# v of the last three layer-1 chunks by seven products for eight, with the sums of its weights made in layer 1's first chunk

## The chip, the cores and the metric

The kernel runs on one core of one Trainium2 chip. The metric is the device time of one execution in microseconds (us). The engines are TensorE (PE, with PEld for its weight loads), VectorE (DVE), ScalarE (ACT), GpSimd (POOL) and SyncE (SP, which here issues most DMAs). They run beside each other, each in its own order, and wait for each other by semaphores.

## What is computed

Two layers share their weights. Each is a dilated local attention (32 heads of 32 channels, 8 positions back in steps of 2), then a SwiGLU block, both with a layer norm ahead and the input added behind. The sizes are 2048 tokens, 1024 channels and 3584 hidden channels, in bf16.

```python
def _A_ref(x, wqkv, wo):
    B, S, D = x.shape
    H = 32; Dh = D // H
    W, dil = 8, 2
    qkv = (lambda x, *d: x.transpose(*d))((x @ wqkv).reshape(B, S, 3, H, Dh), 2, 0, 3, 1, 4)
    q, k, v = qkv[0], qkv[1], qkv[2]
    ...
    logits = jnp.einsum("bhsd,bhswd->bhsw", q, kg) * scale
    logits = jnp.where(mask[None, None, :, :], logits, -1e9)
    attn = _softmax(logits, axis=-1)
    o = jnp.einsum("bhsw,bhswd->bhsd", attn, vg)
    return (lambda x, *d: x.transpose(*d))(o, 0, 2, 1, 3).reshape(B, S, D) @ wo

def _B_ref(x, w1, w3, w2):
    gate = jnp.einsum("bsd,df->bsf", x, w1)
    up = jnp.einsum("bsd,df->bsf", x, w3)
    h = _silu(gate) * up
    return jnp.einsum("bsf,fd->bsd", h, w2)

x = A_x
x = x + _A_ref(_layernorm(x, axis=-1), A_wqkv, A_wo)
x = x + _B_ref(_layernorm(x, axis=-1), B_w1, B_w3, B_w2)
x = x + _A_ref(_layernorm(x, axis=-1), A_wqkv, A_wo)
x = x + _B_ref(_layernorm(x, axis=-1), B_w1, B_w3, B_w2)
```

## The kernel before

**Stages.** The 2048 tokens are cut into four chunks of 512. A pair of layer and chunk is a unit; there are eight, numbered 0 to 7. First q, k and v of all four chunks of layer 0 are computed. Then come the eight units in turn: each has a B stage (the SwiGLU block of its chunk), and behind the B stages of units 1 to 4 stand q, k and v of one chunk of layer 1 (chunk 0 behind unit 1, chunk 3 behind unit 4). Attention itself runs beside this, in half chunks of 256 tokens, nearly all on DVE: score_steps multiplies q and shifted k (L590) and folds the products in a tree (L510 to L514), a softmax follows (L623 to L637), the weights go through POOL's DMA into At, and value_steps does the same with v (L665). Its result oT is multiplied by wo on PE in o_tile (L771, tiles po) and added to x.

**q, k and v.** q_part computes one of the three for one chunk: 64 matmuls with 512 columns into eight PSUM tiles ps (L836), each of which ACT evicts (L840) into a staging tile that goes to DRAM. It takes its weights with a step of eight columns (`t::KT`), which gives the head order that attention wants. Product tiles come from a pool of six PSUM banks; a pool of two more serves po, L and the small size sums.

**Seven products for eight.** In units 2 to 7 w1, w3 and w2 are multiplied by a scheme of Strassen's kind: both factors are cut in half each way, and seven products of sums of the halves replace eight. pipeline (from L1034) does w1 and w3: for each group of weights the products P1, P5, P6, P2 use the tile early and P7, P3, P4 the tile late; P7, P3 and P4 of a group stand between the first products of the next one, and behind the last group the first products of w2 are put between them (`fill`). The pass needs sums of the activations, made on DVE by norm_sums (L298), the last of them in place in xnT; a copy of P1 (L1064), one of P5 (L1069) and one of P6 (L1073) on ACT; and two additions on DVE, L1076 before P3 and L1088 or L1090 before P4.

**Sums of the weights.** They are made once, in units 0 and 1, while w1, w3 and w2 are multiplied in the plain way there. ACT squares each tile for its size (weight_size, L878; for w2 measure2, L958, on pieces loaded in layer 0's q, k and v), a matmul with a tile of ones adds over partitions (L892, L993), scale_of makes a power of two, ACT writes scaled fp16 copies into one of two blocks (L910, L1009), DVE forms the differences (L923, L1015), and POOL's DMA stores them to DRAM (t_d, t2_d). A weight tile is released for the next load when its copies have been queued.

**Order.** The order of PE, DVE, ACT and SP is written out by the program itself, with a clock of its own for each engine (`now`) and a price for each step. Queues hold work for the idle time of an engine: DVE takes from makes, norms, adds, values and scores in background(until), ACT from acts, sizes, parts and reads in act_background. A step is taken when it would end, by these clocks, within the time given. The clocks know of no PSUM banks. Some steps are forced: part_of_w2 takes from the head of `sizes` until all pieces of w2 so far are measured, then loads the next piece; ready_norm and o_tile force norms and attention. The layer norm of units 3 to 7 and of layer 1's chunks 1 to 3 is done by act_norm on ACT (L318 for the moments, then seven small steps on POOL, then L345), and two DMA transposes per half write xnT.

```python
    def act_background():
        for queue in (acts, sizes, parts, reads):
            while True:
                s = head(queue)
                if s is None or max(now["act"], s[1]) + s[0] > now["pe"] + gate[0]:
                    break
                take_act(queue)
```

Weights go through six buffers (wp) in the order of the list `seq`; a buffer is loaded again when it has been released (release, flush).

## Time and profile before

| | |
|---|---|
| median of three runs | 1533.16 us (1532.79 to 1533.34) |
| the profiled execution | 1532.7 us, its span 1531.0 us |
| DVE busy | 1201.8 us, 78% |
| ACT busy | 884.1 us, 58% |
| POOL busy | 153.7 us, 10% |
| granted clock of PE | 1.00 |
| DMA | 439.56 MB, mean 287 GB/s |
| layer 0's q, k and v | 25 to 192 us |
| B stages of units 0 and 1 | 192 to 514 us |
| layer 1's q, k and v | 514 to 556, 701 to 742, 885 to 927, 1073 to 1114 us |

The profile comes from one execution. Its groups give a line, an engine, an operation and tiles (output, arrow, inputs) with the count, the total busy time and the mean of one. The rows of a timeline have the start in us, the length in us, then engine, line and operation; equal neighbours are merged into one row with a count, and idle time ahead stands in brackets with what ended it. The chain of waits is followed back from the last instruction to what released it, and is shown here in order of time. Granted clock 1.00 means that PE was not throttled.

Durations of single operations that the change adds or moves, from the groups: the square of 2048 columns on ACT takes 1.90 us and 0.19 us for its accumulated sum (L878); a scaled copy of 512 columns 0.71 us (L910); a difference of 512 fp16 columns on DVE 0.42 us (L923); a sum of activations 0.69 us (L298); L1076 takes 0.70 us, L1088 0.75 us, an eviction L840 0.59 us.

### The profile page before, as it was taken

The numbers are of one execution on the slowest core, as the hardware profiler recorded it, in microseconds if no ns is written. First come the engines' busy times: TensorE is split into PE (matmuls) and PEld (weight loads), VectorE is DVE, ScalarE is ACT, GpSimd is POOL, SyncE is SP. The second block draws the span as 40 slices with busy tenths as digits, with TensorE's granted clock in tenths as the row PEclk, the third lists the DMA queues.
The fourth block names the chain that finished last, engine by engine and source line by source line (L and its number), as shares of the span: only waits on it lengthen the run. The fifth ranks groups of instructions, "written<-read, shape, count | busy, mean of one in ns | idle before, by whom it ended". The sixth has DMA issues, their size and how long they took to land.

```text
span 1531.0 us, 25095 instructions
## 1 busy us (share of the span) xinstructions
PE 1518.1 (99%) x9594; PEld 989.5 (65%) x9634; DVE 1201.8 (78%) x2126; ACT 884.1 (58%) x1388; POOL 153.7 (10%) x308
## 2 busy tenths in 40 slices
PE   9999999999999999999999999999999999999999
PEld 7666644444444577575786767766677767686865
DVE  4688998889989898989698958898678986435445
ACT  3885476567665357455565564756557445554643
POOL 1210102121211101001011010100111000000000
PEclk9999999999999999999999999999999999999999
DMA  9777969798997888979779997898969988878885
GB/s 321 202 218 215 253 226 330 272 304 289 306 320 247 280 316 294 347 264 303 263 269 324 346 268 282 280 323 302 323 225 333 338 296 282 306 272 334 318 294 203
DMA packets 261432, 439.56 MB, mean 287 GB/s; under 512 B 73856, under 2 KB 201088, under 8 KB 245056
## 3 DMA queue, kind: packets, MB, share of 16 engines
q1 hardware_dynamic: 248464, 390.90, 76.8%
q0 software_dynamic: 12704, 46.93, 8.6%
q8 instruction: 75, 1.23, 0.3%
q14 instruction: 45, 0.37, 0.1%
q10 hardware_dynamic: 144, 0.13, 0.0%
HBM read 345.90 MB, written 67.90 MB: 270 GB/s over the span
## 4 chain that ended last, share of the span: by engine, by line
PE 97%; ACT 1%; issue 1%; DVE 0%; DMA 0%; SPq 0%; ACTq 0%
PE st L1052 32%; PE ps L836 21%; PE w L1165 16%; PE po L771 7%; PE pg L1279 6%; PE pu L1288 6%; PE acc L1310 6%; PE pq L444 1%; PE L L604 0%; DMA wqkv<-in_A_wqkv_dram 0%; ACT L629 0%; ACT L1227 0%; ACT E L629 0%; ACT sg L1227 0%; DVE x_sb L1150 0%
## 5 line engine op out<-in xcount | busy, mean ns | idle before, releaser
L836 PE MATMUL ps<-xnT,wqkv 128*128 128x512 f16 (+1 forms) x1469 | 320.4, 379 | 0.2
L1052 PEld LDWEIGHTS <-early 128*128 128x128 f16 x2688 | 262.6, 98 | 40.4 <-issue 3.5
L836 PEld LDWEIGHTS <-wqkv 128*128 128x128 bf16 x1472 | 210.6, 144 | 108.1 <-issue 2.2
L1165 PE MATMUL w<-t,hT 128*128 128x512 f16 x1008 | 226.0, 379 | 0.6 <-ACT big L1185 0.5
L1052 PEld LDWEIGHTS <-late 128*128 128x128 f16 x2016 | 197.2, 98 | 30.6 <-issue 2.5
L590 DVE TENSOR_TENSOR tree<-qT,kT 128x2048 bf16<-128x2048 bf16 x128 | 156.3, 1221 | 35.8 <-DMA kT<-qkv_d 18.2
L1052 PE MATMUL st<-xnT,late 128*128 128x256 f16 x1344 | 174.2, 273 | 2.2 <-ACT big L1073 2.2
L510 DVE TENSOR_TENSOR tree<-tree 128x1024 bf16<-128x1024 bf16 x256 | 175.6, 686 | 0.9
L1052 PE MATMUL st<-big,early 128*128 128x256 f16 x1344 | 172.3, 273 | 1.6 <-ACT sg L1227 1.1
L1165 PEld LDWEIGHTS <-hT 128*128 128x128 f16 x1008 | 98.2, 98 | 112.9 <-DVE hT L1136 2.0
L1052 PE MATMUL st<-xnT,early 128*128 128x256 f16 x1344 | 165.7, 273 | 0.0
L665 DVE TENSOR_TENSOR tree<-At,vT 128x2048 bf16<-128x2048 bf16 x128 | 156.2, 1221 | 11.9 <-DMA At<-E 10.7
L1064 ACT COPY st<-st 128x512 f32<-128x512 f32 x84 | 48.3, 575 | 128.1 <-PE st L1052 127.4
L771 PE MATMUL po<-wo,oT 128*128 128x512 bf16 x486 | 110.8, 379 | 1.3
L840 ACT CAST hT<-ps 128x512 bf16<-128x512 f32 x96 | 55.8, 585 | 90.6 <-PE ps L836 88.3
L1288 PE MATMUL pu<-xnT,w3t 128*128 128x512 f16 x448 | 105.8, 379 | 0.0
L1279 PE MATMUL pg<-xnT,w1t 128*128 128x512 f16 x448 | 105.8, 379 | 0.0
L1310 PE MATMUL acc<-w2t,hT 128*128 128x512 bf16 x437 | 97.8, 379 | 0.6
L1076 DVE TENSOR_TENSOR st<-st,big 128x512 f32<-128x512 f32 x84 | 58.4, 695 | 46.9 <-ACT big L1073 46.8
L1227 ACT ACTIVATE sg<-st,down_scale 128x512 bf16<-128x512 f32 x126 | 86.6, 687 | 11.6 <-PE st L1052 11.0
L1052 PE MATMUL st<-big,late 128*128 128x256 f16 x672 | 87.1, 273 | 0.0
L771 PEld LDWEIGHTS <-oT 128*128 128x128 bf16 x512 | 50.1, 98 | 55.7
(167 smaller groups left out, 1916.6 us busy)
## 6 DMA issues: line engine op xcount, KB each, us to landing
early<-t_d SPq DMA_DIRECT2D x84, 1024.0 KB, 6.9
late<-t_d SPq DMA_DIRECT2D x84, 768.0 KB, 6.2
t<-t_d SPq DMA_DIRECT2D x42, 1024.0 KB, 7.3
t<-t_d SPq DMA_DIRECT2D x42, 768.0 KB, 5.3
wqkv<-in_A_wqkv_dram SPq DMA_DIRECT2D x28, 1024.0 KB, 8.1
w1t<-in_B_w_dram SPq DMA_DIRECT2D x14, 1024.0 KB, 7.6
w3t<-in_B_w_dram SPq DMA_DIRECT2D x14, 1024.0 KB, 11.0
t_d<-big POOLq DMA_DIRECT2D x28, 512.0 KB, 6.2
```

The costliest lines, as they stand in the source:

```text
L510: nc.vector.tensor_tensor(b, b, buf[:, 4:8, :], op=ALU.add)
L590: V.tensor_tensor(pr, qT[:], kT[:, :, k0:k0 + TCH], op=ALU.mult)
L665: V.tensor_tensor(tm.rearrange("p w (a e) -> p w a e", a=4), At[:].rearrange("p a w e -> p w a e"), win, op=ALU.mult)
L771: nc.tensor.matmul(ps[:], lhsT=oT[:, t, j * P:(j + 1) * P], rhs=wo[:, t, hh * 512:(hh + 1) * 512], start=(t == 0), stop=(t == KT - 1))
L836: nc.tensor.matmul(ps[:], lhsT=ws[kk // KH][:, kk % KH, t::KT], rhs=xnT[:, kk, :], start=(kk == 0), stop=(kk == KT - 1))
L1052: nc.tensor.matmul(out[:, a, :], lhsT=w[:, a, blk, k, :], rhs=rhs[:, k, :], start=start and a == 0 and k == 0, stop=k == KQ - 1, skip_grou ...
L1076: nc.vector.tensor_tensor(G["D"][:], G["D"][:], su, op=ALU.add)
L1165: nc.tensor.matmul(out[:], lhsT=lhs[:, k, j * P:(j + 1) * P], rhs=w[:, k, :], start=start and k == 0, stop=k == nq - 1, skip_group_check=True)
L1227: nc.scalar.activation(sg[:], src, ACTF.Silu, scale=inv)
L1279: nc.tensor.matmul(pg[:], lhsT=w1t[:, kk, fi * P:(fi + 1) * P], rhs=xnT[:, kk, :], start=(kk == 0), stop=(kk == KT - 1))
L1288: nc.tensor.matmul(pu[:], lhsT=w3t[:, kk, fi * P:(fi + 1) * P], rhs=xnT[:, kk, :], start=(kk == 0), stop=(kk == KT - 1))
L1310: nc.tensor.matmul(acc[:], lhsT=hT[:, f, j * P:(j + 1) * P], rhs=tiles[hh][f // nq][:, f % nq, :], start=(f == 0), stop=(f == f1 - f0 - 1))
```

## The change

v of layer 1's chunks 1, 2 and 3 is computed by pipeline, in two groups of four column tiles, instead of by q_part. A new function v_products sets it up: its results are scaled back and staged by ACT (and by L1088 for one quarter) and stored to qkv_d. The new t_dv in DRAM holds the sums of v's weights, and `seq` loads two early and two late tiles where it loaded the two v tiles.

The sums are made in layer 1's chunk 0: its order becomes v, q, k; v's two weight tiles are kept until q is done, and sums_of_v makes 16 scaled copies on ACT and 16 differences on DVE, in the second block and in a third one that lies in hT. Staging of that chunk has four slots for eight. The size of v's weights is measured by size_of_v: four squares queued in `sizes` ahead of q of layer 0's chunk 2, and one size sum. Sums of the activations are now also made for the keys of chunks 1 to 3 (sum_later in queue_q), the one in place only after k. In those chunks the point at which remaining po tiles are forced moves from ahead of v into v's first group.

Two more edits touch units 0 and 1. Sums of w2 are put in `reads` ahead of those of weights that are only prefetched. finish_sums lets DVE work on up to the time at which ACT's next step is ready.

```diff
--- before.py
+++ after.py
@@ -215,14 +215,19 @@
     up_scale = const.tile([P, 2, NG], FP32, name="up_scale")
     down_scale = const.tile([P, 2, NG], FP32, name="down_scale")
     size2 = const.tile([P, 16], FP32, name="size2")
+    size_v = const.tile([P, 4], FP32, name="size_v")
+    down_v = const.tile([P, 1], FP32, name="down_v")
+    up_v = const.tile([P, 1], FP32, name="up_v")
     total = const.tile([P, 1], FP32, name="total")
     down2 = const.tile([P, 1], FP32, name="down2")
     up2 = const.tile([P, 1], FP32, name="up2")
     peak = const.tile([P, 3], FP32, name="peak")
     hsum = const.tile([P, HTN // 2, HT], FP16, name="hsum")
     h16 = hT[:].bitcast(FP16)
+    blocks += [hT[:, 9:16, :].bitcast(FP16).rearrange("p b (k c) -> p b k c", k=KT // 2)]
     t2_d = [dram.tile([P, 7, (b - a) // 2, 512], FP16, name=f"t2_d{i}") for i, (a, b) in enumerate(fsplits)]
     t_d = [[dram.tile([P, 14, KT // 2, P], FP16, name=f"t_d{m}_{g}") for g in range(NG)] for m in range(2)]
+    t_d += [[dram.tile([P, 14, KT // 2, P], FP16, name=f"t_dv_{g}") for g in range(2)]]
     qkv_d = [[dram.tile([P, KT, S], BF16, name=f"qkv_d{l}_{i}") for i in range(3)] for l in range(2)]
 
     def hp():
@@ -692,7 +697,9 @@
             else:
                 seq += [("w2", g0, nq, hh) for hh in range(2) for g0 in (f0, f0 + nq)]
         if 1 <= u and u + 3 < len(units):
-            seq += [("qkv", which, h) for which in range(3) for h in range(2)]
+            seq += [("qkv", which, h) for which in ((2, 0, 1) if u == 1 else (0, 1)) for h in range(2)]
+            if u > 1:
+                seq += [("early", 2, 0), ("early", 2, 1), ("late", 2, 0), ("late", 2, 1)]
     w_tiles, w_at, due, used = [], {}, [], [0]
 
     def load_weight(pieces=1):
@@ -729,7 +736,7 @@
             if rest[0]:
                 got = {}
                 parts.append([weight_size(*rest[0], w, at, got), None])
-                reads.append([weight_sums(*rest[0], w, got), None])
+                reads.append([weight_sums(*rest[0], w, got), None, rest[0]])
         w_at[len(w_tiles)] = at
         w_tiles.append(w)
 
@@ -786,7 +793,8 @@
         key = ("Q", *units[q])
         plain_left.add(key)
         queue_norm(key, units[q][1], range(R))
-        
+        if q > NCH:
+            adds.append([sum_later(key), None])
 
     def sum_later(key):
 
@@ -817,7 +825,7 @@
                 assert norms and head(norms) is not None
         return xnT_at[key]
 
-    def q_part(l, c, which, ws, then=()):
+    def q_part(l, c, which, ws, then=(), last=2, ring=8):
 
         ready = ready_norm(("Q", l, c))
         xnT = xnTs[("Q", l, c)]
@@ -828,7 +836,7 @@
             nc.vector.memset(kT[:, :, 0:HALO], 0.0)
         for t0 in range(0, KT, SG):
             i = (c * 3 + which) * KT // SG + t0 // SG
-            i = i % (7 if l == 0 else 8) * SG
+            i = i % (7 if l == 0 else ring) * SG
             sgt = big[:, i * CH:(i + SG) * CH].bitcast(BF16).rearrange("p (a t) -> p a t", a=SG) if l == 0 else hT[:, i:i + SG, :]
             for t in range(t0, t0 + SG):
                 ps = bank("ps")
@@ -847,16 +855,16 @@
             nc.sync.dma_start(qkv_d[l][which][:, t0:t0 + SG, c * CH:(c + 1) * CH], sgt)
             landed = dma(256, done)
             if l == 0:
-                stored[:] = landed, landed
+                stored[0:2] = landed, landed
             if first and t0 == SG:
                 first_at = load_part(qT, 0, 0, 0, False)
             between(False)
             if t0 // SG < len(then) and then[t0 // SG]:
                 then[t0 // SG]()
         qkv_at[l, c, which] = landed
-        if which == 1:
+        if which == last:
             plain_left.discard(("Q", l, c))
-        if which == 2:
+        if which == last and last != 1 or (l, c, which) == (1, 0, 1):
             xnT_free["Q", l, c] = now["pe"]
         if first:
             qks[0, 0] = qT, kT, max(done + 0.1, first_at)
@@ -913,29 +921,63 @@
             makes.append([differences(m, g, a, now["act"] + 0.1), None])
         made.add((m, g))
 
-    pending, stored, made, held = [0] * 2, [0.0] * 2, set(), []
+    pending, stored, made, held = [0] * 3, [0.0] * 3, set(), []
     junk = hsum[:].bitcast(BF16).rearrange("p k t -> p (k t)")
 
-    def differences(m, g, a, r):
-
-        b = blocks[a]
+    def differences(m, g, a, r, slot=None):
+
+        slot = a if slot is None else slot
+        b = blocks[slot]
         for out, x, y in ((4, 5, 1), (1, 1, 0), (2, 4, 0), (6, 3, 2)):
             yield 0.40, r, lambda: nc.vector.tensor_tensor(
                 b[:, out], b[:, x], b[:, y], op=ALU.add if (x, y) == (4, 0) else ALU.subtract)
-        pending[a] -= 1
+        pending[slot] -= 1
         nc.gpsimd.dma_start(t_d[m][g][:, 4 * a:4 * (a + 1)], b[:, 0:4])
         nc.gpsimd.dma_start(t_d[m][g][:, 8 + 3 * a:8 + 3 * (a + 1)], b[:, 4:7])
-        stored[a] = now["dve"] + 7.0
+        stored[slot] = now["dve"] + 7.0
+
+    got_v = {}
+
+    def size_of_v(i, w, at):
+
+        w_ = w[:].rearrange("p k c -> p (k c)")
+        half = w_.shape[1] // 2
+        for j in range(2):
+            yield 1.95, at, lambda: nc.scalar.activation(junk, w_[:, j * half:(j + 1) * half], ACTF.Square,
+                                                         accum_out=size_v[:, 2 * i + j:2 * i + j + 1])
+        if i == 1:
+            total_scale(size_v, up_v, down_v, got_v)
+
+    def sums_of_v(ws, at):
+
+        while "at" not in got_v:
+            yield "blocked"
+        stored[2] = at
+        for g in range(2):
+            for a in range(2):
+                while pending[1] and pending[2]:
+                    yield "blocked"
+                slot = min((i for i in (1, 2) if not pending[i]), key=lambda i: stored[i])
+                pending[slot] += 1
+                b = blocks[slot]
+                for i, (kh, fh) in ((0, (0, 0)), (1, (0, 1)), (3, (1, 0)), (5, (1, 1))):
+                    t = 4 * g + 2 * fh + a
+                    yield 0.65, max(at, got_v["at"], stored[slot]), lambda: nc.scalar.activation(
+                        b[:, i], ws[kh][:, :, t::KT], ACTF.Copy, scale=up_v[:])
+                makes.append([differences(2, g, a, now["act"] + 0.1, slot), None])
+        made.add("v")
 
     def finish_sums(done):
 
         while not done():
-            if head(reads) is not None:
-                take_act(reads)
-            elif head(parts) is not None:
-                take_act(parts)
+            step = head(reads) or head(parts)
+            if step is not None:
+                background(step[1])
+                take_act(reads if head(reads) is not None else parts)
             elif head(makes) is not None:
-                take(makes)
+                background(head(makes)[1])
+                if head(makes) is not None:
+                    take(makes)
             else:
                 pe_requests(1, True)
 
@@ -1000,7 +1042,7 @@
 
     def sums_of_w2(i, f, ws, loaded):
 
-        while "at" not in got2 or all(pending):
+        while "at" not in got2 or all(pending[0:2]):
             yield "blocked"
         a = min((i for i in range(2) if not pending[i]), key=lambda i: stored[i])
         pending[a] += 1
@@ -1116,6 +1158,42 @@
                     if fill and i == n and tail != "P4":
                         fill(int(tail == "P3"))
             done(i)
+
+    def v_products(l, c):
+
+        key = ("Q", l, c)
+        slots, landed = [0], []
+
+        def stage(G, pair):
+            if ("to", pair) not in G:
+                i = slots[0] % 8 * SG
+                slots[0] += 1
+                G["to", pair] = hT[:, i:i + SG, :]
+                G["left", pair] = 2
+            return G["to", pair]
+
+        def consume(G, q, src, r):
+            pair, t0 = q % 2, HT * (q // 2)
+            to = stage(G, pair)
+            if q != 3:
+                nc.scalar.activation(to[:, :, t0:t0 + HT], src, ACTF.Copy, scale=down_v[:])
+                r = act(0.57, r)
+            G["left", pair] -= 1
+            G["at", pair] = max(r, G.get(("at", pair), 0.0))
+            if not G["left", pair]:
+                t = 4 * G["g"] + 2 * pair
+                nc.sync.dma_start(qkv_d[l][2][:, t:t + SG, c * CH:(c + 1) * CH], to)
+                landed.append(dma(256, G["at", pair]))
+                if len(landed) == 4:
+                    qkv_at[l, c, 2] = max(landed)
+
+        groups = []
+        for g in range(2):
+            G = dict(m=2, g=g, inv=down_v[:])
+            G["corner"] = lambda G=G: stage(G, 1)[:, :, HT:CH]
+            groups.append(G)
+        pipeline(key, groups, consume, lambda i: between(False, i == 0), True)
+        xnT_free[key] = now["pe"]
 
     def products(u, f0, f1, hold):
 
@@ -1316,7 +1394,8 @@
                         release_held(0)
                     if step == 0:
                         steps = range(u * nq // 2, (u + 1) * nq // 2)
-                        reads.extend([sums_of_w2(split, f, tiles, max(times[0] + times[1])), None] for f in steps)
+                        i = next((i for i, item in enumerate(reads) if item[2] not in held), len(reads))
+                        reads[i:i] = [[sums_of_w2(split, f, tiles, max(times[0] + times[1])), None, None] for f in steps]
                     act_background()
                     background(r + 1.0)
                     dve(0.64, r)
@@ -1360,6 +1439,9 @@
                 then = (None, None, lambda: (nc.sync.dma_start(wo[:], wo_v), dma(2048)))
             if c >= 1:
                 then = (then + (None,) * 3)[:3] + (part_of_w2,)
+            if (c, which) == (2, 0):
+                for i in range(2):
+                    sizes.append([size_of_v(i, w_tiles[4 + i], 40.0), None])
             q_part(0, c, which, w_tiles[2 * which:2 * which + 2], then)
             if c == NCH - 1:
                 release(2)
@@ -1375,11 +1457,27 @@
         with_q = 1 <= u and q < len(units)
         b_stage(u, with_q)
         if with_q:
-            for which in range(3):
-                if which == 2:
-                    between(False, True)
-                q_part(*units[q], which, [weight("qkv"), weight("qkv")])
+            if u == 1:
+                for which in (2, 0, 1):
+                    if which == 1:
+                        between(False, True)
+                    ws = [weight("qkv"), weight("qkv")]
+                    if which == 2:
+                        ready = max(w_at[used[0] - 1], now["pe"])
+                        reads.append([sums_of_v(ws, ready), None])
+                    q_part(*units[q], which, ws, (), 1, 4)
+                    if which == 2:
+                        continue
+                    if which == 0:
+                        finish_sums(lambda: "v" in made)
+                        release(2)
+                    release(2)
+                force(makes, lambda: not any(pending))
+                continue
+            for which in range(2):
+                q_part(*units[q], which, [weight("qkv"), weight("qkv")], (), 1)
                 release(2)
+            v_products(*units[q])
 
 
 # ---- launch: one core; inputs and outputs as the reference has them ----
```

## The prediction

> **What bounds the kernel now.** I read the page first, then the chain of waits in order of time, then who waits for whom on PE, and last the timelines of ACT and DVE where the change puts new work. The fences follow that order.
>
> ```profile
> PE 1518.1 (99%) x9594; PEld 989.5 (65%) x9634; DVE 1201.8 (78%) x2126; ACT 884.1 (58%) x1388; POOL 153.7 (10%) x308
> PE 97%; ACT 1%; issue 1%; DVE 0%; DMA 0%; SPq 0%; ACTq 0%
> ```
>
> PE is busy for 1518.1 of 1531.0 us and is 97% of the chain. A matmul taken off PE comes off the end, and a wait put before one goes onto it, nearly one for one. The chain also prices PE (start, length, what), where the spacing of starts counts and not the 379 or 273 ns of a pipelined matmul:
>
> ```profile
> 112.36 27.78 PE ps L836 x128
> ...
> 1072.65 41.44 PE ps L836 x192
> ...
> 1344.74 34.93 PE st L1052 x320
> ```
>
> A 512-column matmul of q, k or v costs 41.44/192 = 0.2158 us, a 256-column one of the seven-product pass 34.93/320 = 0.1092 us. The waits of PE show how little is lost (total, times, longest):
>
> ```profile
> PE st L1052 <- ACT big L1073: 2.2, 1, 2.2
> PE st L1052 <- ACT sg L1227: 1.1, 1, 1.1
> ```
>
> PE waits for no weights after the first 20 us. So ACT, DVE and DMA cost nothing today, and the question is where the change makes one of them late.
>
> ACT in layer 0's q/k/v, where the change puts its measuring:
>
> ```profile
> 122.91 0.58 ACT L840 CAST big<-ps 128x512 bf16<-128x512 f32 x1 [1.14 <-PE ps L836]
> 126.10 1.91 ACT L958 ACTIVATE hsum<-hT 128x2048 bf16<-128x2048 bf16 x1 [2.60 <-DMA hT<-in_B_w_dram]
> ...
> 128.14 1.91 ACT L958 ACTIVATE hsum<-hT 128x2048 bf16<-128x2048 bf16 x1
> ...
> 130.05 2.03 ACT L840 CAST big<-ps 128x512 bf16<-128x512 f32 x4
> ```
>
> Two squares stand between evictions; four products then wait, and PE doesn't. ACT at the end of k in layer 1 (unit 3), with the norm of the next B stage among the evictions:
>
> ```profile
> 913.28 0.58 ACT L840 CAST hT<-ps 128x512 bf16<-128x512 f32 x1
> 913.76 1.24 ACT L345 ACTIVATE xn<-x_sb,mom 128x1024 f16<-128x1024 bf16 x1
> 915.01 0.58 ACT L840 CAST hT<-ps 128x512 bf16<-128x512 f32 x1
> ```
>
> The first line evicts k's last product, the third v's first. L345 lies between at no cost, since v's first product needs 1.73 us.
>
> A seven-product pass starting (unit 5's B stage):
>
> ```profile
> 1113.93 1.04 PE L1052 MATMUL st<-xnT,early 128*128 128x256 f16 x8
> 1114.13 0.58 ACT L840 CAST hT<-ps 128x512 bf16<-128x512 f32 x1 [1.14 <-PE ps L836]
> 1114.80 1.36 PE L1052 MATMUL st<-big,early 128*128 128x256 f16 x11
> ...
> 1115.06 0.57 ACT L1064 COPY st<-st 128x512 f32<-128x512 f32 x1 [0.34 <-PE st L1052]
> ```
>
> P1 starts at 1113.93, P5 at 1114.80. P6 is due 1.75 us after P1 and needs the copy that ends at 1115.63, 1.70 after: 0.05 us of slack.
>
> **What the Trainium skill says.** "PSUM — Partial Sum Buffer", Specifications, gives 8 banks of 512 fp32; this kernel gives six to products, so six unread products stop PE. No run here shows PE stopped by that. "TensorE: Matmul & The Clock Gate", Architectural detail, says that ACT and DVE are strict FIFO; the trace agrees (the four late evictions at 130.05). "SBUF — State Buffer", Door 1, says that each step to a new 16-byte line pays, so reading every eighth bf16 should; the trace agrees for weight loads (144 ns for wqkv's strided tiles, 98 for early's) and shows no such read on ACT.
>
> **The change part by part.**
>
> *Removed and added on PE.* v of three chunks: 64 x 0.2158 = 13.81 us becomes 112 x 0.1092 = 12.23. Three times 1.58 is -4.75 us. One fp32 size matmul is added; the same at L993 shows 2 loads of 190 ns and 2 matmuls of 221: +0.5.
>
> *The measuring.* The change queues four squares of v's weights ahead of the next pair for w2. ACT's order in the built program shows all six together: after the eviction that stands at 122.91 come four squares, then the two L958, then eight evictions. They no longer wait until 126.10 for their data, as v's weights are there. So they start at 122.91 + 0.49 = 123.40; at 2.04 from start to start (126.10 to 128.14), five steps and 1.91 give 135.5, and the first eviction is over at 136.1. PE ends a product every 1.736 us; the one evicted at 122.91 ended at 122.78 (112.36 + 6 x 1.736), and the sixth after it at 133.2. Those six fill the six banks, so PE stands from 133.2 to 136.2: +3.0. PE is the bound from there to the end, and nothing later waits for anything that this time could cover. If the cover were one bank more it would be 1.3.
>
> *Start of the v pass.* ACT's order in all three chunks is: eviction of k's last product, L345, copy of P1 (L1064). With P1's start as zero, that eviction starts at 0.20, L345 runs from 0.68 to 1.92, the copy to 2.49. P6, due at 1.75, starts at about 2.53: 0.8 each, +2.4. Bounds: 0 if L345 is done before k ends, as the trace has it in unit 2 (726.98 to 728.12); 1.5 if its moments from POOL are late.
>
> *End of the v pass.* In a B stage P3 and P4 of a group are spread over the next group's products, and behind the last group w2's P1 fills in. The v pass has only two groups and no fill: P7, P3, P4 follow each other. P4 waits for L1088, which reads P7. Even with DVE free: 0.26 after P7, 0.75 of L1088, 0.05, against 0.87 of P3: 0.2. DVE isn't free in two chunks. Its order has the in-place sum of P7 (L298), which must wait for k's last matmul, then attention, then the adds of the pass and the four sums of the next B stage. With starts spaced as the trace spaces such neighbours (L665 to L512 1.13, L665 to L510 1.25, L510 to L665 0.72, L512 to L510 0.33, L298 to the next 0.6), the last L1088 ends 12.55 us after P1's start in chunk 1 and 13.45 in chunk 3; P4 is due at 13 x 0.873 + 0.8 = 12.15. That is 0.45, 0.2 and 1.35: +2.0. Bounds 0.6 and 4.
>
> *Edits hidden.* In layer 1's first chunk ACT makes 16 scaled copies. Contiguous ones (L910) take 0.71; strided I bound them by 0.71 and 1.4, so 11 to 22 us, and take 0.9. With 16 evictions of 0.585 and one exp of 1.9 that is at most 34 us in the 27.6 of v and q and two po tiles of 3.45: inside, as six banks carry a lag of 8 us; uncovered, the excess would fall on PE. The 16 DVE differences of 0.42 (6.7 us) delay attention, whose po tiles the order moves later too. The eight writes to DRAM on POOL have 100 us before they are read. The loads of unit 2's first weights move behind q's stores on SP, still 13.8 us ahead of use against the page's 6.9. A v pass loads 3.5 MB where 2 MB sufficed: early and late of v are issued a whole pass ahead; the next stage's first early is issued behind the second transpose on SP, some 2 to 4 us into the pass, 9 us before use, which covers the 6.9 by 2 only.
>
> *Reordered queues in units 0 and 1.* Sums of w2 go ahead of those of prefetched weights, DVE work is taken earlier, attention's q/k/v loads on SP come a few places later. The trace has 1 us of PE waits there to win; lost po or weights could cost 3. I take +0.5.
>
> Sum: -4.75 + 0.5 + 3.0 + 2.4 + 2.0 + 0.5 = +3.65 us. The profiled execution took 1532.7 us (span 1531.0 and 1.7 around it), 0.46 below the median 1533.16. So 1536.35 on its own scale, 1536.8 against the median.
>
> **Rivals.**
>
> A, not slower: DVE and ACT arrive early in the v passes, because PE comes 3 us late out of layer 0 while the order of the others was laid out without that hole; only the 0.2 for L1088 stays. -4.75 + 0.6 + 3.0 + 0.5 = -0.65, so 1532.5. It decides if the waits in the three passes sum to less than 1.8 us. For it: attention's results are some 2 us ahead of their po tiles in the trace. Against: L345 and the in-place sum are tied to k's end, not to a clock. 0.24.
>
> B: weights late. If the next stage's first early lands 2 to 3 us behind its use in each of three chunks, 1536.8 + 7 = 1544. For: DMA is 0.9 to 1.1 busy at the ends of these stages. Against: no wait of PE for weights in the whole trace. 0.09.
>
> C: ACT or attention late in units 0 and 1 or the first chunk (strided copies at 1.4, sums late for their release): +3, so 1540. 0.13.
>
> D: neither hole nor waits, 1528.9. It needs the squares to be spread. 0.03.
>
> **How the numbers follow.** The forecast has 0.51, its own range 1535.0 to 1538.8. No change is within 0.2% of 1533.16, that is 1530.1 to 1536.2, about what a measurement of this kernel can tell. The forecast gives 0.35 slower and 0.16 same; B and C 0.22 slower; A 0.22 same and 0.02 faster; D 0.03 faster. In all 0.05 faster, 0.38 same, 0.57 slower. The range 1532.0 to 1540.5 leaves out B, D and the ends.
>
> **What would show it.** PE in layer 0: one wait near 133 of about 3 us, released by an eviction (L840), behind six squares on ACT. In each v pass, P6 waiting for L1064 by 0.8, and the last P4 for L1088 by 0.2 to 1.4. PE's busy time about 4.3 less. Waits of PE on weights would mean B, on pg or po in units 0 and 1 C. No wait at 133 means that my count of banks or squares is wrong; passes of 12.3 us mean A.

## The result, and the profile after

The changed kernel takes 1558.93 us (median of four runs, 1557.54 to 1559.89), the kernel before in the same session 1533.25. The ratio is 1.0166 (95% interval 1.0148 to 1.0183): 25.7 us slower, where +3.65 was forecast. The profiled execution took 1558.95 us, its span is 1557.2. In the code after the change L836 is L844, L840 is L848, L1064 is L1106, L1073 is L1115, L1076 is L1118, L1088 is L1130 and L345 is L350.

The page's line of engines, after:

```profile
PE 1525.1 (98%) x9780; PEld 996.5 (64%) x9780; DVE 1223.8 (79%) x2171; ACT 919.6 (59%) x1424; POOL 158.1 (10%) x316
```

PE has less to do and is busy for longer. The view of what PE waited for, after (total, times, longest):

```profile
PE st L1094 <- DVE st L1118: 4.1, 3, 2.7
PE pu L1366 <- DMA w3t<-in_B_w_dram: 3.6, 1, 3.6
PE st L1094 <- ACT st L1106: 3.0, 3, 1.9
PE ps L844 <- ACT big L848: 2.9, 1, 2.9
PE acc L1388 <- DMA w2t<-in_B_w_dram: 2.4, 2, 1.5
PE st L1094 <- ACT hT L848: 2.0, 1, 2.0
PE po L778 <- DVE x_sb L783: 1.5, 1, 1.5
```

Past its first 20 us the kernel before had two waits over 1 us in this view; now there are these and some smaller ones, two of them on weights. All the waits in this view add up to 28.2 us against 7.0. That isn't all: after some gaps the granted clock of PE is half. Three stretches of the window view, after (PE, PEld, DVE, ACT, POOL busy, then the clock, the DMA share and GB/s):

```profile
120.00:150.00 30.00, 27.12 (x120) 16.43 (x119) 25.43 (x42) 21.76 (x30) 0.00 (x0) 0.94 0.68 191
462.00:484.00 22.00, 17.48 (x69) 7.05 (x67) 16.01 (x28) 15.07 (x22) 5.27 (x9) 0.84 1.07 365
565.00:600.00 35.00, 30.28 (x214) 23.54 (x213) 28.43 (x43) 17.23 (x27) 2.18 (x4) 0.95 1.06 367
```

The clock records show half clock for 3.41 us from 136.2, 6.83 us from 474.2 and 3.41 us from 586.8: 13.65 us at half speed. 1.3 us of them lie inside the wait for w3t, which ends at 475.5, so at most 6.2 us are lost. The kernel before has no such stretch until its end. The account of the span, +26.2: products -4.75 and the size matmul +0.5 (both from the prediction), waits +21.2, half clock +6.2. That is +23.2; about 3 us aren't placed.

By place: the first product of unit 0 is 4.1 us late, layer 1's first chunk 10.9, unit 2's B stage 21.0, and the rest adds 5. So most is lost before unit 2's B stage, where the v passes haven't begun. The delay of the chunk says too little of units 0 and 1: PE has lost some 17 us by then (12.8 in waits, 4.5 in half clock), but 32 matmuls of po that the kernel before did in these units now stand in the chunk, 7 us of it. That chunk takes 52.2 us for 42.1.

The first loss is the forecast one. ACT and PE in layer 0, timelines after:

```profile
122.11 0.59 ACT L848 CAST big<-ps 128x512 bf16<-128x512 f32 x1 [1.14 <-PE ps L844]
122.59 1.92 ACT L946 ACTIVATE hsum<-wqkv 128x2048 bf16<-128x2048 bf16 x1
...
132.78 1.91 ACT L1000 ACTIVATE hsum<-hT 128x2048 bf16<-128x2048 bf16 x1
...
134.69 2.52 ACT L848 CAST big<-ps 128x512 bf16<-128x512 f32 x5
```

```profile
135.31 4.87 PE L844 MATMUL ps<-xnT,wqkv 128*128 128x512 f16 x14 [2.88 <-ACT big L848]
```

Six squares in a row, then the late evictions; PE stands for 2.88 us. The v passes have waits at the start and the end, as forecast, but not of the sizes forecast. Chunk 1 on PE, then chunk 3 on PE and ACT:

```profile
756.57 1.03 PE L1094 MATMUL st<-big,early 128*128 128x256 f16 x8 [1.92 <-ACT st L1106]
...
765.98 1.03 PE L1094 MATMUL st<-big,late 128*128 128x256 f16 x8 [0.50 <-DVE st L1118]
767.77 1.03 PE L1094 MATMUL st<-xnT,late 128*128 128x256 f16 x8 [0.76 <-DVE hT L1130]
```

```profile
1128.98 1.03 PE L1094 MATMUL st<-big,early 128*128 128x256 f16 x8 [0.55 <-ACT st L1106]
...
1139.05 1.03 PE L1094 MATMUL st<-xnT,late 128*128 128x256 f16 x8 [0.30 <-DVE hT L1130]
```

```profile
1126.71 0.59 ACT L848 CAST hT<-ps 128x512 bf16<-128x512 f32 x1
1127.20 1.24 ACT L350 ACTIVATE xn<-x_sb,mom 128x1024 f16<-128x1024 bf16 x1
1128.34 0.59 ACT L1106 COPY st<-st 128x512 f32<-128x512 f32 x1
```

In chunk 3 L350 stands between k's last eviction and P1's copy, and P6 waits for the copy. In chunk 1 ACT has also waited 1.38 us for the moments of that norm from POOL.

### The profile page after: what moved, and what is told of

Read it like the earlier page. It is cut to its first block, busy times and chain, and to the rows that moved or that the text cites. A ratio compares the mean times of both kernels' runs of the same rounds, so it can differ in the third digit from the quotient of the medians.

```text
span 1557.2 us, 25585 instructions
## 1 busy us (share of the span) xinstructions
PE 1525.1 (98%) x9780; PEld 996.5 (64%) x9780; DVE 1223.8 (79%) x2171; ACT 919.6 (59%) x1424; POOL 158.1 (10%) x316
## 4 chain that ended last, share of the span: by engine, by line
PE 50%; DVE 10%; DMA 5%; ACT 4%; issue 2%; POOL 0%; DVEq 0%; ACTq 0%; POOLq 0%
PE st L1094 28%; PE w L1243 13%; PE po L778 5%; PE ps L844 4%; DVE tree L670 2%; DMA t_d<-big 2%; DVE tree L515 1%; DVE tree L595 1%; DMA w3t<-in_B_w_dram 1%; DMA xnT<-xn 1%; DMA late<-t_d 1%; DMA At<-E 1%; DVE tree L517 1%; DVE hT L1214 1%; DVE big L932 0%
## 5 line engine op out<-in xcount | busy, mean ns | idle before, releaser
L1094 PEld LDWEIGHTS <-early 128*128 128x128 f16 x2880 | 282.0, 98 | 44.5 <-issue 3.8
L844 PE MATMUL ps<-xnT,wqkv 128*128 128x512 f16 (+1 forms) x1280 | 281.4, 381 | 2.9 <-ACT big L848 2.9
L844 PEld LDWEIGHTS <-wqkv 128*128 128x128 bf16 x1280 | 183.4, 144 | 98.5 <-issue 7.3
L1094 PEld LDWEIGHTS <-late 128*128 128x128 f16 x2160 | 211.3, 98 | 40.1 <-issue 8.8
L1094 PE MATMUL st<-xnT,late 128*128 128x256 f16 x1440 | 187.1, 273 | 3.0 <-DVE hT L1130 1.3
L1094 PE MATMUL st<-big,early 128*128 128x256 f16 x1440 | 185.5, 273 | 3.0 <-ACT st L1106 3.0
L1094 PE MATMUL st<-xnT,early 128*128 128x256 f16 x1440 | 176.7, 273 | 2.0 <-ACT hT L848 2.0
L778 PE MATMUL po<-wo,oT 128*128 128x512 bf16 x512 | 116.2, 379 | 2.8 <-DVE x_sb L783 1.5
L1106 ACT COPY st<-st 128x512 f32<-128x512 f32 x90 | 51.8, 575 | 105.9 <-PE st L1094 105.0
L1118 DVE TENSOR_TENSOR st<-st,big 128x512 f32<-128x512 f32 x90 | 62.6, 696 | 48.4 <-ACT big L1115 48.3
L1094 PE MATMUL st<-big,late 128*128 128x256 f16 x720 | 93.7, 273 | 4.1 <-DVE st L1118 4.1
L1366 PEld LDWEIGHTS <-w3t 128*128 128x128 bf16 x448 | 44.1, 99 | 57.6 <-DMA w3t<-in_B_w_dram 4.1
```

The costliest lines, as they stand in the source:

```text
L778: nc.tensor.matmul(ps[:], lhsT=oT[:, t, j * P:(j + 1) * P], rhs=wo[:, t, hh * 512:(hh + 1) * 512], start=(t == 0), stop=(t == KT - 1))
L844: nc.tensor.matmul(ps[:], lhsT=ws[kk // KH][:, kk % KH, t::KT], rhs=xnT[:, kk, :], start=(kk == 0), stop=(kk == KT - 1))
L1094: nc.tensor.matmul(out[:, a, :], lhsT=w[:, a, blk, k, :], rhs=rhs[:, k, :], start=start and a == 0 and k == 0, stop=k == KQ - 1, skip_grou ...
L1118: nc.vector.tensor_tensor(G["D"][:], G["D"][:], su, op=ALU.add)
L1366: nc.tensor.matmul(pu[:], lhsT=w3t[:, kk, fi * P:(fi + 1) * P], rhs=xnT[:, kk, :], start=(kk == 0), stop=(kk == KT - 1))
```

## The experiments

"The plan" is the program's own clocks and prices, by which it writes out the order of the engines. Theories: T1, the two queue edits reorder units 0 and 1 and make weights late. T2, the squares in layer 0 cost by the stall, the half clock and the shift behind it. T2', the measuring costs because it moves the plan's clocks, whatever the instructions take. T3, making v's sums in layer 1's first chunk costs. "The chunk" below is that chunk.

**Queue edits and squares, each undone or done alone.** e1 is the kernel before with the first two of these edits; e2 takes them out of the changed kernel; e3 has the third; e4 is e2 and e3 together.

```diff
-                        reads.extend([sums_of_w2(split, f, tiles, max(times[0] + times[1])), None] for f in steps)
+                        i = next((i for i, item in enumerate(reads) if item[2] not in held), len(reads))
+                        reads[i:i] = [[sums_of_w2(split, f, tiles, max(times[0] + times[1])), None, None] for f in steps]
...
-            if head(reads) is not None:
-                take_act(reads)
+            step = head(reads) or head(parts)
+            if step is not None:
+                background(step[1])
+                take_act(reads if head(reads) is not None else parts)
...
-            if (c, which) == (2, 0):
-                for i in range(2):
-                    sizes.append([size_of_v(i, w_tiles[4 + i], 40.0), None])
+            if (c, which) == (3, 0):
+                then = (square, square, square, part_of_w2)
+            if (c, which) == (3, 1):
+                then = (square, None, None, part_of_w2)
```

> The kernel before with the change's two queue edits alone: background work before each step of the routine that finishes the sums, and the w2 sums put ahead of those weights' sums that are not held. Nothing of v is added. T1 (the queue edits put unit 1's w3t squares ahead of the w2 copies, so that weights come late in unit 1's second split and the clock halves there): 1541 to 1545 us, with PE standing some 4 us for w3t near 470 us of the span. T2 (the squares of v's weights in layer 0 start the loss: a hole of 2.9 us, half clock for 3.4 us, and everything after them shifted against the transfers): 1532.5 to 1534.5, no gap over 1 us in unit 1.

> The changed kernel with both queue edits undone. T1: unit 1's second split runs as before, its 9 us come back, 1547 to 1550 us. T2: the gap for w3t stays, 1557 to 1560. T3 (the making of v's sums in layer 1's first chunk costs most) says nothing on the queues: 1555 to 1559.

> The changed kernel with the four squares of v's weights taken one at a time, one after each second pair of blocks of q's and k's parts of layer 0's chunk 3, and not four in a row. T2: the gap of 2.9 us near 132 us and the half clock after it go (4.6 us), and unit 1's 9 us with them if it was the shift that put w3t late: 1545 to 1548. T1: only the 4.6 us: 1553.5 to 1555.5.

> Both of the last two: squares spread, queue edits undone. T1 and T2 each 1541 to 1545, since what either blames is gone; what then stands above the kernel before is the making of the sums in layer 1's first chunk (3 to 5 us, with the half clock after it) and whatever moved besides, less what the seven products save. If the losses do not add, over 1548.

e1: 1532.71 us, ratio 0.9997 (0.9989 to 1.0006). This run says less than it seems to: in the kernel before the queue edits leave every instruction where it was, so e1 is the same program once more. What they do in the changed kernel is seen in e4, where undoing them gives another order. e3: 1558.24 (ratio 1.0161). The stall at 132 us is gone, unit 0 starts at 191.7 us instead of 196.6, and everything is lost again by the end, so T2 falls as well. e4: 1557.74, so the loss is there with the queue edits and without them, and T1 falls. e2, which nobody had expected: 1672.26 (ratio 1.0901). The largest part stands in the chunk, where PE waits some 60 us for DVE: the differences of v's weights stand on DVE before attention's work, and DVE waits for ACT (timeline of e2). Another 22 us PE waits in units 0 and 1 for an ACT step (sg, L1359), which wasn't followed further.

```profile
591.88 1.68 DVE L932 TENSOR_TENSOR hT<-hT 128x512 f16<-128x512 f16 x4 [21.12 <-ACT hT L965]
```

The same undoing cost nothing in e4, with the squares elsewhere. Whether an order is good depends on everything else in the plan.

**Measuring apart from the sums.** e5 takes the measuring out and leaves v's scale a constant 32, so it doesn't follow the data; e6 also gives the strided copies their true price; e7 and e8 are the kernel before with the queue edits and the measuring alone, in a row or spread.

```diff
-    got_v = {}
+    got_v = {"at": 0.0}
+    nc.vector.memset(up_v[:], 32.0)
+    nc.vector.memset(down_v[:], 0.03125)
...
-                    yield 0.65, max(at, got_v["at"], stored[slot]), lambda: nc.scalar.activation(
+                    yield 1.26, max(at, got_v["at"], stored[slot]), lambda: nc.scalar.activation(
```

> The changed kernel without the measuring of v's weights: no squares, no size matmul, the scale of v's sums is the constant 32. Left out: the data-dependent scale. Up to layer 1's first chunk its instructions stand in the order of the kernel before. T2' (the four squares and the size matmul move the planner's clocks, so that it orders units 0 and 1 otherwise and the weights of unit 1 come late there): the 10.9 us that the changed kernel is late at layer 1's first chunk all come back, and no half clock near 474 us; 1545 to 1549 us. T1' (the weights of unit 1 are late for another reason): the gap near 470 us stays, over 1553. T3 (making the sums in layer 1's first chunk): what stays above the kernel before arises between 513 and 620 us of the span, 10 us or more.

> The last one with the strided copies of v's weights priced in the order-making plan at 1.26 us, what the profile shows, and not at 0.65. The instructions are the same, their order in layer 1's first chunk is not. T3a (the loss there is a plan made with a price that is half the real one: 16 copies, 10 us too few on ACT): the order fits, PE's waits of unit 2's first B stage go, 3 to 6 us under the last one. T3b (the work itself, 20 us of ACT and the differences on DVE in a stage of 42 us, is too much for the stage): within 2 us of the last one.

> The kernel before with the queue edits and the measuring of v's weights as the change does it (four squares in a row, the size matmul, the scale), whose result nobody uses. T2 and T2': at layer 1's first chunk some 11 us late, as the changed kernel is, and about that at the end: 1542 to 1546 us. If the changed kernel's loss in unit 1 needs v's products too: 1536 to 1538 (the hole and the half clock after it alone).

> The last one with the squares one at a time in layer 0's chunk 3. T2' (any change of the planner's clocks costs): no hole in layer 0, but unit 1's order is moved as in the changed kernel with spread squares, so 1541 to 1547. T2 (the hole is the cause): 1533 to 1535.

e5: 1539.39 (1.0040, 1.0025 to 1.0055), below what was expected. e6: 1532.85 (1.0003, 0.9994 to 1.0011), 6.5 under e5, where 3 to 6 was expected; PE's wait for DVE's addition in unit 2's B stage falls from 4.2 to 2.25 us and doesn't go. e7: 1553.66 (1.0136), e8: 1552.14 (1.0123), both above. So the measuring, which nobody uses in e7 and e8, costs some 20 us, and all of v's sums and products cost 6.3 us, or nothing with a true price. e7 also shows that unit 2's late start needs no strided copy: its B stage is 13.3 us late against the kernel before, of which the chunk has added 6.9.

The price, in groups of equal form, after (the last numbers: total, mean ns, idle before):

```profile
L918 ACT ACTIVATE big<-w3t,up_scale 128x512 f16<-128x512 bf16 x56 | 36.4, 711 | 19.6 <-DMA t_d<-big 18.0 <-DVE up_scale L878 1.6
...
L965 ACT ACTIVATE big<-wqkv,up_v 128x512 f16<-128x512 bf16 x8 | 9.9, 1272 | 0.0
L965 ACT ACTIVATE hT<-wqkv,up_v 128x512 f16<-128x512 bf16 x8 | 9.8, 1254 | 2.6 <-DMA t_dv<-hT 2.6
```

A copy that reads every eighth bf16 takes 1.26 us, one that reads neighbours 0.71, and the plan charges 0.65 and 0.61. Sixteen copies make ACT 10 us later than the plan thinks, and the differences behind them hold up DVE. PE after, at the start of unit 2:

```profile
577.33 1.05 PE L1094 MATMUL st<-xnT,early 128*128 128x256 f16 x8 [2.00 <-ACT hT L848]
...
586.34 1.46 PE L1094 MATMUL st<-big,late 128*128 128x256 f16 x8 [2.72 <-DVE st L1118]
```

**The plan apart from the instructions.** e9 keeps the whole plan of e7 and emits neither squares nor size matmul nor scale: it is the kernel before in another order, which is e7's. e10 does the reverse in the changed kernel. e11 is the changed kernel with 1.26 alone. e12 is the whole change, squares spread and unknown to the plan, with 1.26.

```diff
-            yield 1.95, at, lambda: nc.scalar.activation(junk, w_[:, j * half:(j + 1) * half], ACTF.Square,
+            yield 1.95, at, lambda: None
...
-            yield 1.95, at, lambda: nc.scalar.activation(junk, w_[:, j * half:(j + 1) * half], ACTF.Square,
+            yield 0.0, 0.0, lambda: nc.scalar.activation(junk, w_[:, j * half:(j + 1) * half], ACTF.Square,
```

> The measuring of v's weights in the plan alone: the order of all instructions is that of the run with the measuring in a row (1553.7 us), but the four squares, the size matmul and the five small DVE operations are not there. It is the kernel before, computing the same, in another order. If the order is the cause of what is lost in units 0 and 1: 1545 to 1551 us, with PE standing for w3t near 465 us of the span. If the squares and the stall and half clock that they bring are the cause: 1533 to 1536.

> The other half: the changed kernel with the four squares in a row and v's size real, but unknown to the plan, so that all else stands in the order of the run without measuring (1539.4 us). v's size goes through w2's size matmul (20 columns for 16). If the order is the cause: 1539.4 plus a stall in layer 0 of at most 2.9 and a half clock of at most 1.7, 1539.5 to 1544. If the squares are the cause: 1552 to 1559.

> The changed kernel with the strided copies priced at 1.26 us in the plan, and nothing else. If the losses of the measuring and of the price are independent: 1558.9 less the 6.5 us that the price was worth without measuring, 1551 to 1554. If the price was worth 6.5 us only in that order: anywhere from 1548 to 1560.

> The whole change, complete, with both mended: the four squares one at a time in layer 0's chunk 3 and unknown to the plan, the strided copies at 1.26. If the order is the cause, as without measuring and with the true price (1532.9 us): 1531.5 to 1534.5, the same as the kernel before or 0.1% under it. If the squares cost by themselves: 1536 to 1541. Faster than 1530.1 (0.2%) would mean that the v passes save their whole 4.75 us, which the last runs do not show.

e9: 1551.27 (1.0120, 1.0106 to 1.0133): 18 us slower without one added instruction. e10: 1540.48 (1.0051), 1.1 over e5: the squares themselves cost next to nothing (here four and two stand apart on ACT, and PE doesn't stall). e11: 1549.43 (1.0113), below the range for independent losses and inside the wider one. e12: 1535.40 (1.0020, 1.0011 to 1.0030), above its range and under that of the other theory. Its order is e6's but for the squares and the small DVE operations; near 215 us PE waits 2.77 us for such an operation (down_scale, L892), with half clock behind, which e6 doesn't. Of e9's 16 us (spans of the two traces), 9.1 are lost before unit 2's B stage and 6.9 in it. PE's two largest waits in e9 stand in these two places:

```profile
PE st L1070 <- DVE st L1094: 4.7, 1, 4.7
PE pu L1306 <- DMA w3t<-in_B_w_dram: 3.6, 1, 3.6
```

How an order makes weights late is seen in unit 1, at the second of them. SyncE's queue, before:

```profile
395.14 8.70 SPq L272 DMA_TRANSPOSE xnT<-xn  x4
...
409.68 4.05 SPq L727 DMA_DIRECT2D w1t<-in_B_w_dram  x1
413.83 3.29 SPq L727 DMA_DIRECT2D w3t<-in_B_w_dram  x1
```

and in e9:

```profile
382.70 17.32 SPq L725 DMA_DIRECT2D w2t<-in_B_w_dram  x2
402.53 12.44 SPq L275 DMA_TRANSPOSE xnT<-xn  x4
...
423.88 3.41 SPq L730 DMA_DIRECT2D w3t<-in_B_w_dram  x1
```

The load of w3t starts 10 us later, of which 2.6 are the delay of the whole stage. SyncE's order is nearly the same in both; its loads wait longer for their buffers. ACT, before:

```profile
435.22 1.33 ACT L1009 ACTIVATE big<-w2t,up 128x512 f16<-128x512 bf16 x2 [1.06 <-DVE x_sb L1324]
436.46 1.89 ACT L878 ACTIVATE hsum<-w3t 128x2048 bf16<-128x2048 bf16 x1
```

and in e9:

```profile
437.70 1.91 ACT L881 ACTIVATE hsum<-w3t 128x2048 bf16<-128x2048 bf16 x1 [9.39 <-DMA w3t<-in_B_w_dram]
...
441.64 4.99 ACT L1027 ACTIVATE big<-w2t,up 128x512 f16<-128x512 bf16 x8
```

The squares of w3t, a tile loaded ahead, stand before twelve of the sixteen copies of w2; in the kernel before fourteen of these come first. ACT waits 9.39 us for w3t with those copies behind it, the buffers come free late, and so does the next load. PE, in e9:

```profile
468.09 1.90 PE L1306 MATMUL pu<-xnT,w3t 128*128 128x512 f16 x8 [3.57 <-DMA w3t<-in_B_w_dram]
```

**Which entry of the plan.** The orders that the program writes out show it: 7.8 us charged to ACT for the squares leave the order as it was but for a few places on ACT, and the size matmul's slot on PE leaves it as it was. The 1.1 us charged to DVE for v's scale, alone, change everything behind; 1.0 alone still gives the old order on all engines but DVE, 0.9 on DVE too. Beside the squares' charge 0.9 already gives e9's order, and 0.2 doesn't. The five operations take 0.93 us in the trace (142.49 to 143.42 after). e13 charges 1.1 us to DVE in the kernel before with the queue edits and does nothing else; e14 is the changed kernel with 0.2; e15 is e14 with 1.26; e16 is e9 with the two squares of that w3t held back.

```diff
+        yield 0.0, 0.0, lambda: makes.insert(0, [iter([(1.1, now["act"] + 2.5, lambda: None)]), None])
...
-            yield 1.1, r, emit
+            yield (1.1 if n == 16 else 0.2), r, emit
...
-                parts.append([weight_size(*rest[0], w, at, got), None])
+                parts.append([weight_size(*rest[0], w, at + (9.0 if rest[0] == (1, 4) else 0.0), got), None])
```

> The kernel before with the queue edits, and 1.1 us charged once to VectorE in the plan, where the scale of v's weights would be made; no instruction is added, none left out. That charge alone gives another order of the instructions in units 0 and 1; a charge of 0.9 us, or 7.8 us charged to ScalarE for the squares, gives the order of the kernel before but for some places of single ScalarE instructions. If any order that comes from a shifted plan is worse than the tuned one: 1540 to 1555. If only the order of the last plan-only run is bad: 1531 to 1537.

> The changed kernel with one number of the plan changed: the five small VectorE operations that make v's scale are charged at 0.2 us and not at 1.1. All the instructions of the change are there. The SyncE and GpSimd orders become those of the run without measuring. If the loss in units 0 and 1 comes from this flip: 1539.4 and the hole with its half clock, 1540 to 1545. If the squares in a row matter beyond the hole: over 1550.

> The changed kernel with two numbers of the plan changed: the item of the last run at 0.2, and the strided copies at 1.26 us. If the two losses are what separates the changed kernel from the kernel before: 1532.9 (no measuring, true price) and at most 4.6 for the hole and the half clock after it, 1533 to 1538. If something else is lost: over 1541.

> The plan-only run (1551.3 us) with the two squares of the w3 weights of unit 1's second split held back in the plan by 9 us, so that they do not stand ahead of the w2 copies on ScalarE. If the strict order on ScalarE (copies behind squares behind a transfer that lands late) makes the weights of that split late: its PE gap of 3.6 us near 465 us goes, and 5 to 8 us with it, 1543 to 1547. If the transfers are late by themselves: 1550 to 1552. It moves other things too, so a number over 1552 would say nothing of this link.

e13: 1554.21 (1.0136, 1.0121 to 1.0152). Its order isn't that of e9, and its waits are others (PE in e13):

```profile
PE po L771 <- DVE down_scale L884: 5.1, 1, 5.1
PE po L771 <- DVE oT L514: 3.1, 4, 1.7
PE st L1058 <- DVE big L298: 2.5, 1, 2.5
PE acc L1316 <- DMA w2t<-in_B_w_dram: 2.5, 1, 2.5
```

Unit 2's B stage begins 20.5 us late here. So it isn't one bad order: another one that comes from a shifted plan is as bad. e14: 1543.64 (1.0078). One number takes 15 us off the changed kernel. Its order is e5's but for the added squares and small operations; it is 4.3 us over e5, and the stall of layer 0 is 2.87 of them. e15: 1539.01 (1.0038, 1.0024 to 1.0051), a little above its range. Two numbers take 20 us off. But 0.2 is no truer than 1.1. With 0.93, which is what the trace shows, and 1.26 for the copies, the program writes e11's order, instruction for instruction, and e11 took 1549.43. The 0.2 helps because it is too small to move the order. PE's waits in e15:

```profile
PE ps L844 <- ACT big L848: 2.9, 1, 2.9
PE st L1094 <- ACT big L1115: 2.2, 1, 2.2
PE st L1094 <- DVE st L1118: 1.8, 1, 1.8
```

The first is the stall of layer 0; no wait on w2t or w3t is left among the large ones. e16: 1544.23 (1.0076), 7.0 us under e9, and the wait for w3t isn't there any more. The squares ahead of the copies were that link, as far as one run tells that also moves other things.

**Towards a faster version.** In e6 ACT waits 4.56 us in the chunk for a store of v's part, which SyncE issues behind four transposes and four weight loads. e17 (e12) and e18 (e6) issue these stores from GpSimd.

```diff
-            nc.sync.dma_start(qkv_d[l][which][:, t0:t0 + SG, c * CH:(c + 1) * CH], sgt)
+            (nc.gpsimd if (l, c, which) == (1, 0, 2) else nc.sync).dma_start(
+                qkv_d[l][which][:, t0:t0 + SG, c * CH:(c + 1) * CH], sgt)
```

> The mended whole change (1535.4 us) with the four stores of v's part of layer 1's first chunk issued by GpSimd and not by SyncE, where they stand behind four transposes and four weight loads. If ScalarE's wait of 4.56 us for such a store is what makes VectorE late in unit 2's first B stage: PE's wait of 2.2 us there goes, and its half clock where there is one, 1531 to 1534. If VectorE is late by its own backlog: 1534.5 to 1536.5. Worse than 1537 would mean that GpSimd's queue, which also stores v's sums, is now the late one.

> The same store edit on the run without measuring and with the true price (1532.9 us), v's scale being the constant 32. First theory: 1529 to 1531.5, under the kernel before. Second: 1532 to 1534.

e17: 1534.98 (1.0020, 1.0013 to 1.0028). e18: 1533.20 (1.0001, 0.9993 to 1.0009). ACT no longer waits for the store (in e18 it waits 2.05 us for one of v's sums instead), but PE's wait for L1118's add only falls from 2.2 to 1.3 us (e12, e17) and 1.8 (e6, e18), and the times stay where they were. The store was part of DVE's lateness there; that the rest is DVE's own backlog was not traced. No version here beats the kernel before. From layer 1's chunk 1 to the end e6 is 2.9 us shorter than the kernel before, of the 4.75 taken off; unit 2's B stage before it gives 3.2 back.

## Why the prediction was wrong

**"Reordered queues in units 0 and 1 ... I take +0.5", bounds -1 to +3.** This step failed. It named the queue edits, and alone these move nothing (e1); with the squares spread, undoing them gains nothing (e4). It didn't ask what the measuring does to the order: a price added to the plan can move every decision behind it. The charge of 1.1 us on DVE for v's scale alone gives an order that costs 22 us, 20 of them before unit 2's B stage (e13); the measuring's whole charge costs 18, of which 9 are lost by then and 7 in that stage (e9). It read the new order only around the new instructions, not what else had moved in units 0 and 1, where the squares of w3t now stood ahead of twelve copies of w2. The rival C, with "sums late for their release", had this kind of lateness and its place, at +3 and 0.13, about a sixth of its size.

**"Edits hidden": nothing for the chunk.** Its bounds of 0.71 and 1.4 for a strided copy held the measured 1.26. But 0.9 was taken, and the sum on ACT was set against PE's time in the chunk as a whole. The plan's own price, 0.65, wasn't compared with it. The error of 10 us on ACT falls on the differences and the attention behind them on DVE. Mended, it is worth 6.5 us without measuring (e5, e6), 9.5 in the changed kernel (e11) and 4.6 beside the other number (e14, e15). These gains include what the new order brings, which the runs don't part from the price's own share.

**Not in the sum at all: the clock after a stall.** At most 6.2 us in the changed kernel, 1.7 of them behind the stall in layer 0.

**The stall in layer 0, +3.0.** Right: 2.88, released by an eviction behind six squares. The Trainium skill's "PSUM — Partial Sum Buffer", Specifications, had given the banks of which this kernel uses six, and the trace now shows PE stopped by them.

**Start and end of the v pass, +2.4 and +2.0.** Near in the sums, not in the parts, so in part luck. P6 waited 1.92, 0.55 and 0.55 us, 3.0 in all, where 0.8 each was said; the 1.92 is the case of late moments from POOL, bounded there by 1.5. P4 waited for L1130 (L1088 before) 0.76, 0.22 and 0.30, which is 1.3 of the 2.0; another 1.4 are waits of P3 for L1118 in chunks 1 and 2 (0.50, 0.87), which the sum didn't have. This is a matter of order too. In e6 chunk 3's L350 stands one eviction earlier, and its pass has no wait over 0.2 us: there the prediction's lower bound for the start, 0, holds. "PE's busy time about 4.3 less" was no test: the page has 7.0 more. Half clock counts as busy, which explains up to 6.2 of the difference of 11.3; the rest isn't placed.

**The products, -4.75.** Never seen alone. In e6, which has neither the size matmul nor half clock before its end, PE is busy 3.7 us less than before (1514.4 of the span), and the stretch from chunk 1 on is 2.9 shorter, its own waits in it. So most of the term is there.

What stays open: which decision the 1.1 us flip first, why DVE is late for unit 2's B stage in e9, and whether the kernel before holds the best order or only a good one. The last 5 us of the changed kernel after unit 2's start are its v passes and smaller waits, not traced one by one.

## What to carry to other kernels

Where a program writes its own order by prices, an added step has two costs, that of its instructions and that of the order it brings, and the second can be many times the first. It can be measured: charge the plan without the instructions, and emit the instructions without the charge. When a tuned order must be kept, compare the new order with the old one far from the edit too. A price from a trace helps where it was far off, as for the strided copies; it doesn't make the order safe, as the 0.93 us of v's scale show.

## What the hardware showed that was not expected

The granted clock falls to half for 3.41 us, or 6.83, after gaps of PE much shorter than that, and not each time: in e12 after a gap of 2.24 us, in e9 not after one of 3.57. Each trace is one execution; e12's, with 1539.46 us, is among the slowest of its ten. The same gap of 2.20 us near 1175 us was followed by half clock in e12, e15 and e18 and not in e6 and e17. The Trainium skill, "TensorE: Matmul & The Clock Gate", Part 1 (the HAM clock gate), says that the clock gate goes to half after an idle window of about 3.4 us, 3413 ns, and that the window is free-running. The lengths and the dependence on chance agree; that the gap must be as long as the window doesn't: 2.2 us was enough, by this profile's modelled ends of matmuls. Half clock that falls inside the gap costs nothing: in the changed kernel the stretch of 6.83 us begins 1.3 us before its gap of 3.58 us ends. By these traces a stall of 2 to 4 us costs from nothing to some 2.8 us ((6.83 - 1.3) / 2) on top of itself.
